# The last 128 rows of a gate's weights: in two early transfers of 16 partitions each, instead of in a late one of 128

## The chip, the cores and the metric

One core of a Trainium2 chip runs the kernel alone. The metric is the device time of one execution in microseconds (us), and lower is better. The core has five engines that compute or issue (TensorE, VectorE, ScalarE, GpSimd, SyncE) and 16 DMA engines that move data between the chip's memory (HBM) and the core's on-chip memory (SBUF, 128 partitions). Three runs of the kernel before took 242.82, 243.05 and 243.05 us; the median is 243.05 us.

## The reference

One decode step of a transformer block for four sequences (B = 4, one token each, D = 512), all in float32. A condition vector `c` sets six modulation vectors through one weight matrix `w_mod` (512 x 3072):

```python
mod = (_silu(c) @ w_mod).reshape(c.shape[0], 6, 1, -1)
sa, ca, ga, sb, cb, gb = (mod[:, 0], mod[:, 1], mod[:, 2], mod[:, 3], mod[:, 4], mod[:, 5])
h = _layernorm(x, axis=-1) * (1 + ca) + sa
x = x + ga * _A_ref(h, A_k_cache, A_v_cache, A_wq, A_wo)
h = _layernorm(x, axis=-1) * (1 + cb) + sb
x = x + gb * _B_ref(h, B_w1, B_w3, B_w2)
```

`_A_ref` is attention of 32 query heads over 8 key/value heads and a window of the last 2048 cached positions; `_B_ref` is the gated feed-forward layer `(silu(h @ w1) * (h @ w3)) @ w2` with 1792 hidden units. The gate `gb`, the last of the six, is what the change is about: `gb = silu(c) @ w_mod[:, 2560:3072]`, a product over 512 rows of weights that is needed only at the very end.

## The kernel before, in words

The kernel reads about 101 MB once and keeps nothing between executions. Nearly all of it comes in as transfers over all 128 partitions, issued by SyncE (`load`, L88) in an order written out by hand (L91 to L125). Each transfer has its own place in two big buffers `KV[0]`, `KV[1]` (128 x 16384 floats) and one smaller one, `WP`.

- **Start.** SyncE issues `t0_in` (the 16 columns of `c`, and the weights of `sa` and `ca`) into `T0`, which is the front of `KV[1]`; ScalarE's queue issues the first query weights `t1_in` and the 8 KB of `x_in`; SyncE then issues the keys and values of the first group, `KV[0]`. GpSimd writes constants with memsets (L128 to L139). VectorE and ScalarE make the layer norm of `x` and `silu(c)` (L174 to L188); the result `sc` is a 128 x 16 tile, four columns for each of the four blocks of 128 rows of `c`. TensorE multiplies it with `T0` (L302 to L306). When that is done (semaphore `pe` at 1) `KV[1]` is free and SyncE issues the second group's keys and values (L95, L96).
- **Attention.** TensorE, ScalarE and VectorE go through the eight groups two by two (L317 to L343). SyncE waits for the end of a group's work on a buffer (`x_done`, `qt_done`, `a_done`) before it issues the next transfer into it (L97 to L116).
- **Tail.** When the seventh group is done, SyncE issues the weights of `ga`, `sb`, `cb` (`wm_in`, L118) and a part of the feed-forward weights (L119). When the eighth is done it issues, one behind the other (L120 to L125), the rest of `w3` in two transfers, `gb_in` (the weights of `gb`, 512 rows laid out as 128 partitions x 4 blocks of 512 columns, 1024 KB) and `w2` in six transfers, cut so that the last ones are small (`W2_CUTS`, L18). TensorE computes `ga`, `sb`, `cb` (L380 to L385), then the feed-forward layer, and in between `gb` (L453 to L456): four products of a 128 x 4 block of `sc` with 128 x 512 weights, each into its own 32 rows of the bank `bM`. They are summed over the four blocks by a later product with `same` (L471 to L477). The last products with `w2` (L462 to L486), two VectorE operations (L488, L490) and a store (L492) end the kernel.

The bank `bM` is written three times: for `sa` and `ca`, for the attention's output (L353), which VectorE reads at L390, and for `gb`.

Of the kernel before, what the change touches and what calls it, by code (L numbers as in the profile page):

```python
# [5 lines left out]
AF = mybir.ActivationFunctionType  # L6
# [4 lines left out]
B, D, HQ, G, SK, DH, W, FF = 4, 512, 32, 8, 8192, 128, 2048, 1792  # L11
P = 128
# [2 lines left out]
EPS = 1e-5  # L15
CHUNKS = [(j, c) for c in range(4) for j in range(4) if c < 2 or j < 3]
HEAD = 8
W2_CUTS = [0, 4, 8, 10, 12, 13, 14]  # L18
PAIRS = G // 2

# [20 lines left out]
        return (self.sem, self.n)  # L41


def block_kernel(nc, x_in, t0_in, t1_in, kv_in, w_in, wm_in, f1_in, f2_in, gb_in, w2_in, out):
    T, v, s, gp, S = nc.tensor, nc.vector, nc.scalar, nc.gpsimd, nc.sync

    def sems(names):
        return [nc.alloc_semaphore(n) for n in names.split()]

    def sb(name, cols, rows=P):  # L50
        return nc.alloc_sbuf_tensor(name, (rows, cols), F32).ap()

    def bank(name):
        return nc.alloc_psum_tensor(name, (P, 512), F32).ap()

    (first,) = sems("first")
    A = Queue(nc, s, "act")
    V = Queue(nc, v, "dve")
    L = Queue(nc, gp, "pool")
    dx, dt0, dt1, dkv, dk, dva, dvb, dwo, dm, df1, df2a, df2b, dgb = sems("dx dt0 dt1 dkv dk dva dvb dwo dm df1 df2a df2b dgb")  # L60
    dw = sems(" ".join(f"dw{i}" for i in range(len(W2_CUTS) - 1)))
    z_ok, q_ok, p_ok, k_ok, va_ok, vb_ok, pt_ok, o_ok, ot_ok = sems("z_ok q_ok p_ok k_ok va_ok vb_ok pt_ok o_ok ot_ok")
    s_done, q_done, qt_done, pp_done, o_done, x_done, a_done, pe, last = sems("s_done q_done qt_done pp_done o_done x_done a_done pe last")
# [1 line left out]

    KV = [sb("KV0", 16384), sb("KV1", 16384)]
    WP = sb("WP", 8192)
    T0 = KV[1][:, : 16 + 4096]
    x_sb = sb("x_sb", 512, B)
    ident, same, eps = sb("ident", P), sb("same", B), sb("eps", 1)  # L70
    sc, e1, e2 = sb("sc", 16), sb("e1", 16), sb("e2", 16)
    hT, h2T = sb("hT", 16), sb("h2T", 16)
    Z = sb("Z", B * 28)
    q_sb, p_sb, o_sb, a_sb, y_sb, g_sb, u_sb, gb_sb = [sb(n, 512) for n in "q_sb p_sb o_sb a_sb y_sb g_sb u_sb gb_sb".split()]
# [10 lines left out]
    bS, bQ, bT, bP, bO, bX, bA, bM = [bank(n) for n in "bS bQ bT bP bO bX bA bM".split()]  # L85


    def load(dst, src, sem):  # L88
        S.dma_start(dst, src).then_inc(sem, 16)  # L89

    load(T0, t0_in, dt0)  # L91
    s.dma_start(WP[:, 4096:], t1_in).then_inc(dt1, 16)
# [27 lines left out]
    S.wait_ge(x_done, G)  # L120
    load(KV[1][:, :3072], f2_in[:, :3072], df2a)
    load(KV[1][:, 3072:6144], f2_in[:, 3072:], df2b)
    load(KV[1][:, 6144:8192], gb_in, dgb)
    for a, b, sem in zip(W2_CUTS[:-1], W2_CUTS[1:], dw):
        load(KV[1][:, 8192 + a * 512 : 8192 + b * 512], w2_in[:, a * 512 : b * 512], sem)  # L125


    l_eps = L.op(gp.memset(eps, EPS))  # L128
    t = L.op(gp.memset(ident, 0.0))
    L.wait(t)  # L130
# [48 lines left out]
    v_same = V.op(v.tensor_reduce(same, ident.rearrange("p (j i) -> p i j", i=32)[:, :B, :], axis=AX.X, op=ALU.add))  # L179

    A.wait((dt0, 16))
    t = A.op(s.activation(e1, T0[:, :16], AF.Exp, scale=-1.0))
    V.wait(t)
    t = V.op(v.tensor_scalar(e2, e1, 1.0, None, op0=ALU.add))
    V.wait(t)
    t = V.op(v.reciprocal(e2, e2))
    V.wait(t, (dt0, 16))
    t_sc = V.op(v.tensor_mul(sc, T0[:, :16], e2))  # L188

    A.wait((pe, 1))  # L190
    t_sa = A.op(s.copy(sa_sb, bM[32 : 32 + B, :]))
# [1 line left out]
    t = V.op(v.scalar_tensor_tensor(xs, bM[:B, :], 1.0, xc, op0=ALU.add, op1=ALU.mult))  # L193
# [60 lines left out]
    def mm(o, lhsT, rhs, start=True, stop=True):  # L254
        return T.matmul(o, lhsT, rhs, start=start, stop=stop, skip_group_check=True)  # L255
# [46 lines left out]
    T.wait_ge(V.sem, t_sc[1])  # L302
    for k in range(4):
        for i in range(2):
            ins = mm(bM[32 * i : 32 * i + B, :], sc[:, k * B : (k + 1) * B], T0[:, 16 + (2 * k + i) * 512 : 16 + (2 * k + i + 1) * 512], k == 0, k == 3)
    ins.then_inc(pe, 1)  # L306
    T.wait_ge(V.sem, t_h[1])
    for k in range(4):
        ins = T.transpose(bT[:, k * B : (k + 1) * B], h[:, k * P : (k + 1) * P], ident[:B, :B])
# [71 lines left out]
    for k in range(4):  # L381
        for i in range(3):
            at = (3 * k + i) * 512
            ins = mm(bX[32 * i : 32 * i + B, :], sc[:, k * B : (k + 1) * B], KV[0][:, at : at + 512], k == 0, k == 3)
# [3 lines left out]

    V.wait((pe, 3), t_ga)
    t = V.op(v.tensor_mul(ag, bM[:B, :], ga_sb))  # L390
    V.wait(t)
    t_x1 = V.op(v.scalar_tensor_tensor(x1, ag, 1.0, x_sb, op0=ALU.mult, op1=ALU.add, accum_out=st2[:, 0:1]))
    t_ss, t_r0, t_xc = stats(x1, t_x1, st2)
# [10 lines left out]
    for k in range(4):  # L404
        ins = T.transpose(bT[:, k * B : (k + 1) * B], h[:, k * P : (k + 1) * P], ident[:B, :B])
# [4 lines left out]
    def view(t_):  # L410
        return t_.rearrange("p (c j i) -> p c j i", c=4, j=4)
# [4 lines left out]
    for k in range(4):  # L416
        for j in range(4):
            at = 6144 + k * 2048 + j * 512
            ins = mm(bQ[32 * j : 32 * j + B, :], h2T[:, k * B : (k + 1) * B], KV[0][:, at : at + 512], k == 0, k == 3)
# [3 lines left out]
    for k in range(4):  # L423
# [5 lines left out]
        for j in range(3):  # L429
            at = k * 1536 + j * 512  # L430
            ins = mm(bA[32 * j : 32 * j + B, :], h2T[:, k * B : (k + 1) * B], KV[1][:, at : at + 512], k == 0, k == 3)
    ins.then_inc(pe, 1)
    A.wait((pe, 7))
    t = A.op(s.activation(view(eT), view(bP)[:, :, :, :B], AF.Exp, scale=-1.0))
    V.wait(t)
    t = V.op(v.tensor_scalar(dT, eT, 1.0, None, op0=ALU.add))
    V.wait(t)
    t = V.op(v.reciprocal(rT, dT))
# [7 lines left out]
    for c in range(4):  # L446
        ins = T.transpose(bS[:, c * P : c * P + 96], u_sb[:96, c * P : (c + 1) * P], ident[:96, :96])
# [3 lines left out]


    T.wait_ge(dgb, 16)  # L453
    for k in range(4):
        ins = mm(bM[32 * k : 32 * k + B, :], sc[:, k * B : (k + 1) * B], KV[1][:, 6144 + 512 * k : 6144 + 512 * (k + 1)])
    ins.then_inc(pe, 1)  # L456
    A.wait((pe, 10))
    t_gb = A.op(s.copy(gb_sb, bM))
    T.wait_ge(V.sem, t_hid[1])
    hw = view(hidT)  # L460
    w2 = KV[1][:, 8192 : 8192 + 14 * 512].rearrange("p (n m) -> p n m", n=14)
    for i in range(len(W2_CUTS) - 1):  # L462
        T.wait_ge(dw[i], 16)
        for n in range(W2_CUTS[i], W2_CUTS[i + 1]):
            jj, c = CHUNKS[n]
            if n < HEAD:
                ins = mm(bO[32 * (n % 4) : 32 * (n % 4) + B, :], hw[:, c, jj, :], w2[:, n, :], n < 4, n >= HEAD - 4)
                continue
            for j in range(4):
                ins = mm(bX[32 * j : 32 * j + B, :P], hw[:, c, jj, :], w2[:, n, j * P : (j + 1) * P], n == HEAD, n == 13)  # L470
        if i == 0:  # L471
            T.wait_ge(A.sem, t_gb[1])
            for j in range(4):
                ins = mm(bT[32 * j : 32 * j + B, :P], same, gb_sb[:, j * P : (j + 1) * P])
# [13 lines left out]
    t = V.op(v.tensor_mul(yt, bX[:, :P], gbJ))  # L488
# [8 lines left out]
def _layout(i):  # L497
    import numpy as np

    def a(t):  # L500
        return np.ascontiguousarray(t)

    k = i["A_k_cache"][:, :, SK - W :, :].reshape(B, G, NT, 512, DH)
    v = i["A_v_cache"][:, :, SK - W :, :].reshape(B, G, NT, 4, P, DH)
    k = k.transpose(1, 4, 2, 0, 3).reshape(G, P, 8192)
    v = v.transpose(1, 4, 2, 0, 3, 5).reshape(G, P, 8192)
    wm = i["w_mod"].reshape(4, P, 6, 512).transpose(1, 0, 2, 3)
    c = i["c"].reshape(B, 4, P).transpose(2, 1, 0).reshape(P, 16)
    wq = i["A_wq"].reshape(4, P, G, 512).transpose(2, 1, 0, 3).reshape(G, P, 2048)
    wo = i["A_wo"].reshape(G, R, P, D).transpose(0, 2, 1, 3).reshape(G, P, 2048)  # L510
    pairs = [[wo[2 * p], wo[2 * p + 1]] + ([wq[2 * p + 2], wq[2 * p + 3]] if p < 3 else [wo[6], wo[7]]) for p in range(4)]
    w1 = i["B_w1"].reshape(4, P, FF).transpose(1, 0, 2)
    w3 = i["B_w3"].reshape(4, P, FF).transpose(1, 0, 2)
    w2 = i["B_w2"].reshape(14, P, D)
    return {
        "x_in": a(i["A_x"].reshape(B, D)),
        "t0_in": np.concatenate([c, wm[:, :, 1::-1].reshape(P, 4096)], 1),
        "t1_in": np.concatenate([wq[0], wq[1]], 1),
        "kv_in": np.concatenate([k, v], 2),
        "w_in": np.stack([np.concatenate(p, 1) for p in pairs]),  # L520
        "wm_in": a(wm[:, :, 2:5]).reshape(P, 6144),
        "f1_in": np.concatenate([w1, w3[:, :, 1536:]], 2).reshape(P, 8192),
        "f2_in": a(w3[:, :, :1536]).reshape(P, 6144),
        "gb_in": a(wm[:, :, 5]).reshape(P, 2048),
        "w2_in": a(np.stack([w2[4 * j + c_] for j, c_ in CHUNKS], 1)).reshape(P, 14 * D),
    }

# [14 lines left out]
```

## Time and profile before

| | before |
|---|---|
| median of 3 runs | 243.05 us (242.82 to 243.05) |
| the profiled execution's own time | 243.12 us |
| its span, first to last instruction | 241.8 us |
| bytes moved by DMA | 101.33 MB, mean 419 GB/s over the span |
| TensorE busy with products | 136.2 us (56%) |
| VectorE, ScalarE, GpSimd busy | 38.6, 25.1, 1.7 us |
| mean granted TensorE clock | 0.852 |

The profiled execution took 1.3 us more than its span, and 0.07 us more than the median of the runs. A page of the profile has the busy shares of each engine, the chain of work that ended last, the costliest groups of instructions and the DMA queues; the trace can be asked for the same in any stretch of time. A DMA share of 1.00 in a stretch means 16 DMA engines busy all the time; transfers are counted where a packet starts, so that short stretches may read a little over 1. Queue q1 is SyncE's, q10 ScalarE's; the queues of the kind "instruction" carry the instructions themselves. The profile doesn't tell the 16 DMA engines apart.

### The profile page before, as it was taken

What the parts mean: (1) busy time and instruction counts of PE and PEld (TensorE: products, weight loads), DVE (VectorE), ACT (ScalarE), POOL (GpSimd) and SP (SyncE); (2) the same over time, 40 slices, a digit from 0 to 9 for tenths busy, and PEclk for the clock granted to TensorE, in tenths of its full rate; (3) what the DMA queues carried; (4) which work ended last, traced back from release to release, by engine and by line L of the source; (5) the groups of instructions that cost most, each with busy time, mean ns of one, the idle gap of its engine ahead of it and who ended that gap; (6) DMA issues with size and microseconds to landing.
All of it is one profiled execution on the core that took longest, in us unless ns stands there. A gap on an engine that the chain in (4) does not pass through costs nothing. (4 is left out here: it accounts for less than half of the span.)

```text
span 241.8 us, 2271 instructions
## 1 busy us (share of the span) xinstructions
PE 136.2 (56%) x940; PEld 37.3 (15%) x940; DVE 38.6 (16%) x126; ACT 25.1 (10%) x54; POOL 1.7 (1%) x14
## 2 busy tenths in 40 slices
PE   3004677817660387276723772667237768665964
PEld 0000121201210012112200121112001222111211
DVE  3003202202200022022000220220002222124122
ACT  2002002100120002001100020001001201123110
POOL 2000000000000000000000000000000000000000
PEclk9999959967996579987985798879858997995999
DMA  7998989899989898999898989998989999999992
GB/s 266 451 500 369 499 371 488 379 417 445 493 379 488 369 499 381 407 428 510 369 499 369 499 369 423 434 510 369 499 350 442 442 400 440 453 431 396 418 411 106
DMA packets 4044, 101.33 MB, mean 419 GB/s; under 512 B 452, under 2 KB 580, under 8 KB 1096
## 3 DMA queue, kind: packets, MB, share of 16 engines
q1 hardware_dynamic: 3888, 99.17, 95.6%
q10 hardware_dynamic: 152, 2.11, 2.1%
q8 instruction: 3, 0.05, 0.1%
q14 instruction: 1, 0.01, 0.0%
HBM read 101.20 MB, written 0.07 MB: 419 GB/s over the span
## 5 line engine op out<-in xcount | busy, mean ns | idle before, releaser
L255 PE MATMUL bS<-KV,Z 128*16 128x512 f32 x256 | 42.5, 824 | 38.8 <-PEq L258 38.8
L255 PE MATMUL bO<-KV,pT 128*16 128x512 f32 x256 | 31.9, 642 | 0.5
L255 PEld LDWEIGHTS bS<-KV,Z 128*16 128x16 f32 x256 | 9.1, 122 | 66.6 <-issue 66.6
L218 DVE TENSOR_REDUCE MX<-bS 128x1 f32<-128x512 f32 x8 | 5.5, 691 | 79.6 <-PE bS L255 79.6
L255 PE MATMUL bM<-KV,sc 128*4 128x512 f32 x24 | 7.3, 835 | 16.6 <-DVE sc L188 16.6
L367 ACT ACTIVATE p_sb<-bS,NB 128x512 f32<-128x512 f32 x8 | 5.5, 687 | 101.2 <-ACTq L358 101.2
L276 PE MATMUL bP<-ident,p_sb 128*128 128x128 f32 x32 | 5.0, 280 | 17.3 <-PEq L258 17.3
L255 PE MATMUL bA<-WP,oT 128*4 128x512 f32 x64 | 10.4, 728 | 5.2 <-PEq L258 5.2
L255 PEld LDWEIGHTS bO<-KV,pT 128*16 128x16 f32 x256 | 8.1, 105 | 22.9 <-issue 22.9
L372 ACT ACTIVATE o_sb<-bO,LB 128x512 f32<-128x512 f32 x8 | 5.5, 687 | 48.7 <-ACTq L358 48.7
L255 PE MATMUL bQ<-WP,hT 128*4 128x512 f32 x64 | 9.2, 648 | 0.6 <-DVE hT L197 0.6
L276 PE MATMUL bX<-ident,o_sb 128*128 128x128 f32 x32 | 5.0, 280 | 7.9 <-PEq L258 7.9
L244 DVE TENSOR_REDUCE oT<-bX 128x16 f32<-128x64 f32 x8 | 1.8, 224 | 44.0 <-PE bX L276 44.0
L276 PE MATMUL bT<-ident,q_sb 128*128 128x128 f32 x32 | 5.5, 298 | 3.6 <-PEq L258 3.6
L276 PEld LDWEIGHTS bP<-ident,p_sb 128*128 128x128 f32 x32 | 3.4, 140 | 24.4 <-issue 24.4
L276 PEld LDWEIGHTS bX<-ident,o_sb 128*128 128x128 f32 x32 | 3.4, 141 | 15.0 <-issue 15.0
L227 DVE COPY pT<-bP 128x256 f32<-128x256 f32 x8 | 3.4, 424 | 13.7 <-PE bP L276 13.7
L255 PE MATMUL bQ<-KV,h2T 128*4 128x512 f32 x32 | 5.3, 831 | 0.3 <-DVE h2T L408 0.3
L276 PEld LDWEIGHTS bT<-ident,q_sb 128*128 128x128 f32 x32 | 3.7, 150 | 8.3 <-issue 8.0
L255 PEld LDWEIGHTS bM<-KV,sc 128*4 128x4 f32 x24 | 1.0, 106 | 22.6 <-DVE sc L188 18.2
L255 PE MATMUL bX<-KV,sc 128*4 128x512 f32 x24 | 4.4, 592 | 0.0
L202 DVE TENSOR_REDUCE Z<-bT 128x16 f32<-128x64 f32 x8 | 1.8, 224 | 15.4 <-PE bT L276 15.1
(101 smaller groups left out, 68.0 us busy)
## 6 DMA issues: line engine op xcount, KB each, us to landing
WP<-w_in SPq DMA_DIRECT2D x3, 4096.0 KB, 18.9
KV<-kv_in SPq DMA_DIRECT2D x1, 4096.0 KB, 24.1
KV<-f_in SPq DMA_DIRECT2D x1, 4096.0 KB, 25.9
KV<-kv_in SPq DMA_DIRECT2D x1, 3072.0 KB, 30.9
KV<-wm_in SPq DMA_DIRECT2D x1, 3072.0 KB, 16.5
KV<-f_in SPq DMA_DIRECT2D x2, 1536.0 KB, 17.2
KV<-t_in SPq DMA_DIRECT2D x1, 2056.0 KB, 12.3
WP<-t_in ACTq DMA_DIRECT2D x1, 2048.0 KB, 12.5
```

What stands on the lines that cost most here:

```text
L202: v.tensor_reduce(Z.rearrange("p (b i) -> p b i", b=B)[:, :, 12 : 12 + R], bT.rearrange("p (r k i) -> p i r k", r=R, k=4)[:, :B], axis=AX. ...
L218: t = V.op(v.reduce_max(MX[:, 0:1], bS, axis=AX.X))
L227: v.tensor_copy(pT.rearrange("p (t b c r) -> p c b t r", t=NT, b=B, c=4), bP.rearrange("p (c b i) -> p c b i", c=4, b=B)[:, :, :, :16].rea ...
L244: V.op(v.tensor_reduce(oT.rearrange("p (r b) -> p r b", r=R), diag, axis=AX.X, op=ALU.add), ot_ok)
L255: return T.matmul(o, lhsT, rhs, start=start, stop=stop, skip_group_check=True)
L276: ins = T.transpose(dst[:, c * P : (c + 1) * P], src[:, c * P : (c + 1) * P], ident)
L367: A.op(s.activation(p_sb, bS, AF.Exp, bias=NB[:, 0:1], accum_out=SM[:, 0:1]), p_ok)
L372: A.op(s.mul(o_sb, bO, LB[:, 0:1]), o_ok)
```

## The change

The weights of `gb` have four blocks of 128 rows. The first three stay in `gb_in`, which is now 768 KB. The last block's 128 rows are cut into four sub-blocks of 32 rows, laid side by side (32 partitions x 2048 columns), and put on partitions 16 to 31 and 64 to 79 of a new tile `GC` (80 partitions x 2048 columns), the rest of which GpSimd sets to zero. GpSimd's own queue issues this at the start of the kernel, as two transfers of 16 partitions each (128 KB each). The source of each is written as four rows of four (of an array that has a fifth, unused row, so that the two can't be merged into one of sixteen). Ahead of them and behind them stands a transfer of 4 x 2 floats into an unused tile `GZ`.

The matching values of `c` are added to `t0_in`: 16 columns more (`cs`), zero outside those 32 partitions, so that `sc` has 32 columns. The four products with `GC` are placed behind those with `w_mod`'s middle part, into `bM`, after VectorE has read the attention's output from it. The three products that are left at the old place add to them. `w2` moves forward by 512 columns in `KV[1]`.

```diff
+SUB = 4
+BANDS = [16, 64]
+ROWS = [p for at in BANDS for p in range(at, at + 16)]
+C_IN = 16 + 4 * SUB
+W2_AT = 6144 + 1536
...
+    GC, GZ = sb("GC", SUB * 512, 80), sb("GZ", 4, 4)
+    T0 = KV[1][:, : C_IN + 4096]
...
-    load(KV[1][:, 6144:8192], gb_in, dgb)
+    load(KV[1][:, 6144:7680], gb_in, dgb)
...
+    t = L.op(gp.memset(GC, 0.0))
+    L.wait(t)
+    gp.dma_start(GZ[:, :2], gc_in[0, :4, :2]).then_inc(dgc, 16)
+    for e, at in enumerate(BANDS):
+        gp.dma_start(GC[at : at + 16], gc_in[4 * e : 4 * e + 4, :4]).then_inc(dgc, 16)
+    gp.dma_start(GZ[:, 2:], gc_in[0, :4, :2]).then_inc(dgc, 16)
     l_eps = L.op(gp.memset(eps, EPS))
...
-    t = A.op(s.activation(e1, T0[:, :16], AF.Exp, scale=-1.0))
+    t = A.op(s.activation(e1, T0[:, :C_IN], AF.Exp, scale=-1.0))
...
     t = V.op(v.tensor_mul(ag, bM[:B, :], ga_sb))
+    T.wait_ge(V.sem, t[1])
+    T.wait_ge(dgc, 64)
+    for m in range(SUB):
+        mm(bM[32 * m : 32 * m + B, :], sc[:80, 16 + m * B : 16 + (m + 1) * B], GC[:, m * 512 : (m + 1) * 512], True, m == 3)
...
     T.wait_ge(dgb, 16)
-    for k in range(4):
-        ins = mm(bM[32 * k : 32 * k + B, :], sc[:, k * B : (k + 1) * B], KV[1][:, 6144 + 512 * k : 6144 + 512 * (k + 1)])
+    for k in range(3):
+        ins = mm(bM[32 * k : 32 * k + B, :], sc[:, k * B : (k + 1) * B], KV[1][:, 6144 + 512 * k : 6144 + 512 * (k + 1)], False, True)
...
+    cs = np.zeros((P, SUB * B), c.dtype)
+    cs[ROWS] = i["c"].reshape(B, 512)[:, 384:].reshape(B, SUB, 32).transpose(2, 1, 0).reshape(32, SUB * B)
+    gc = np.zeros((8, 5, SUB * 512), c.dtype)
+    gc[:, :4] = i["w_mod"][384:, 5 * 512 :].reshape(SUB, 32, 512).transpose(1, 0, 2).reshape(8, 4, SUB * 512)
...
-        "gb_in": a(wm[:, :, 5]).reshape(P, 2048),
+        "gb_in": a(wm[:, :3, 5]).reshape(P, 1536),
+        "gc_in": gc,
```

Where the four products stand: TensorE's rows there before, from the products with `wm_in` to those of the feed-forward layer (tile out<-in, size, and the semaphores waited for).

```order
L255 MATMUL bX<-KV,sc 4x512 [waits dm]
L255 MATMUL bX<-KV,sc 4x512 x11
L405 MATMUL bT<-ident,h 128x4 [waits dve]
L405 MATMUL bT<-ident,h 128x4 x3
L255 MATMUL bQ<-KV,h2T 4x512 [waits df1,dve]
```

And the same place now:

```order
L267 MATMUL bX<-KV,sc 4x512 [waits dm]
L267 MATMUL bX<-KV,sc 4x512 x11
L267 MATMUL bM<-GC,sc 4x512 [waits dgc,dve]
L267 MATMUL bM<-GC,sc 4x512 x3
L421 MATMUL bT<-ident,h 128x4 [waits dve]
L421 MATMUL bT<-ident,h 128x4 x3
L267 MATMUL bQ<-KV,h2T 4x512 [waits df1,dve]
```

The four products, with a wait for `GC` (`dgc`) and for VectorE's reading of `bM`, stand between the two groups that followed each other before.

GpSimd's first rows before, behind its four built-in constants:

```order
L128 MEMSET eps 128x1
L129 MEMSET ident 128x128
```

And now:

```order
L134 MEMSET GC 80x2048
L136 DMA GZ<-gc_in 4x2
L138 DMA GC<-gc_in 16x1x2048 x2
L139 DMA GZ<-gc_in 4x2
L140 MEMSET eps 128x1
L141 MEMSET ident 128x128
```

One long memset and four transfers now stand ahead of every constant that GpSimd writes.

More of the change, by code (lines that the diff above doesn't have):

```diff
@@ L41, in op, with block_kernel @@
         return (self.sem, self.n)
-def block_kernel(nc, x_in, t0_in, t1_in, kv_in, w_in, wm_in, f1_in, f2_in, gb_in, w2_in, out):
+def block_kernel(nc, x_in, t0_in, t1_in, kv_in, w_in, wm_in, f1_in, f2_in, gb_in, gc_in, w2_in, out):
     T, v, s, gp, S = nc.tensor, nc.vector, nc.scalar, nc.gpsimd, nc.sync
@@ L59, in block_kernel @@
     L = Queue(nc, gp, "pool")
-    dx, dt0, dt1, dkv, dk, dva, dvb, dwo, dm, df1, df2a, df2b, dgb = sems("dx dt0 dt1 dkv dk dva dvb dwo dm df1 df2a df2b dgb")
+    dx, dt0, dt1, dkv, dk, dva, dvb, dwo, dm, df1, df2a, df2b, dgb, dgc = sems("dx dt0 dt1 dkv dk dva dvb dwo dm df1 df2a df2b dgb dgc")
     dw = sems(" ".join(f"dw{i}" for i in range(len(W2_CUTS) - 1)))
@@ L67, in block_kernel @@
     WP = sb("WP", 8192)
-    T0 = KV[1][:, : 16 + 4096]
+    GC, GZ = sb("GC", SUB * 512, 80), sb("GZ", 4, 4)
+    T0 = KV[1][:, : C_IN + 4096]
     x_sb = sb("x_sb", 512, B)
     ident, same, eps = sb("ident", P), sb("same", B), sb("eps", 1)
-    sc, e1, e2 = sb("sc", 16), sb("e1", 16), sb("e2", 16)
+    sc, e1, e2 = sb("sc", C_IN), sb("e1", C_IN), sb("e2", C_IN)
     hT, h2T = sb("hT", 16), sb("h2T", 16)
@@ L122, in block_kernel @@
     load(KV[1][:, 3072:6144], f2_in[:, 3072:], df2b)
-    load(KV[1][:, 6144:8192], gb_in, dgb)
+    load(KV[1][:, 6144:7680], gb_in, dgb)
     for a, b, sem in zip(W2_CUTS[:-1], W2_CUTS[1:], dw):
-        load(KV[1][:, 8192 + a * 512 : 8192 + b * 512], w2_in[:, a * 512 : b * 512], sem)
+        load(KV[1][:, W2_AT + a * 512 : W2_AT + b * 512], w2_in[:, a * 512 : b * 512], sem)
+    t = L.op(gp.memset(GC, 0.0))
[4 more added lines that the diff above has]
+    gp.dma_start(GZ[:, 2:], gc_in[0, :4, :2]).then_inc(dgc, 16)
     l_eps = L.op(gp.memset(eps, EPS))
@@ L187, in block_kernel @@
     V.wait(t, (dt0, 16))
-    t_sc = V.op(v.tensor_mul(sc, T0[:, :16], e2))
+    t_sc = V.op(v.tensor_mul(sc, T0[:, :C_IN], e2))
     A.wait((pe, 1))
@@ L304, in block_kernel @@
         for i in range(2):
-            ins = mm(bM[32 * i : 32 * i + B, :], sc[:, k * B : (k + 1) * B], T0[:, 16 + (2 * k + i) * 512 : 16 + (2 * k + i + 1) * 512], k == 0, k == 3)
+            ins = mm(bM[32 * i : 32 * i + B, :], sc[:, k * B : (k + 1) * B], T0[:, C_IN + (2 * k + i) * 512 : C_IN + (2 * k + i + 1) * 512], k == 0, k == 3)
     ins.then_inc(pe, 1)
@@ L460, in block_kernel @@
     hw = view(hidT)
-    w2 = KV[1][:, 8192 : 8192 + 14 * 512].rearrange("p (n m) -> p n m", n=14)
+    w2 = KV[1][:, W2_AT : W2_AT + 14 * 512].rearrange("p (n m) -> p n m", n=14)
     for i in range(len(W2_CUTS) - 1):
@@ L516, in _layout @@
         "x_in": a(i["A_x"].reshape(B, D)),
-        "t0_in": np.concatenate([c, wm[:, :, 1::-1].reshape(P, 4096)], 1),
+        "t0_in": np.concatenate([c, cs, wm[:, :, 1::-1].reshape(P, 4096)], 1),
         "t1_in": np.concatenate([wq[0], wq[1]], 1),
```

## The prediction

> **What bounds the kernel now.** I read the page's DMA part first, since so much is moved, then the chain that ended last, then the last microseconds in short windows.
>
> ```profile
> DMA  7998989899989898999898989998989999999992
> ...
> DMA packets 4044, 101.33 MB, mean 419 GB/s; under 512 B 452, under 2 KB 580, under 8 KB 1096
> ...
> q1 hardware_dynamic: 3888, 99.17, 95.6%
> ...
> q8 instruction: 3, 0.05, 0.1%
> q14 instruction: 1, 0.01, 0.0%
> ```
>
> The first row is the busy share of the 16 DMA engines in 40 slices: no slice but the first and the last falls under 8 tenths. TensorE is busy 56% of the span, so this kernel is bound by its transfers. The q1 row gives an engine's pace: 99.17 MB in 0.956 x 241.8 us x 16 engine-microseconds is 26.8 KB a microsecond (thousand bytes) for one engine. So 16,384 B cost an engine 0.61 us, 32,768 B 1.22 us.
>
> Do the engines ever run dry in the middle? SyncE waits for TensorE before most issues, but the issues are early. The page's issue rows give the time from issue to landing:
>
> ```profile
> WP<-w_in SPq DMA_DIRECT2D x3, 4096.0 KB, 18.9
> ...
> KV<-gb_in SPq DMA_DIRECT2D x1, 1024.0 KB, 20.8
> ...
> KV<-kv_in SPq DMA_DIRECT2D x7, 32.3
> ```
>
> 4,096 KB take 16 engines 9.8 us at that pace, and landed after 18.9: such a transfer stood some 9 us behind others. The queue holds many microseconds of work at each issue, so TensorE's speed doesn't matter there. What counts is how many bytes each engine has to move until the end. The chain says the same of the end:
>
> ```profile
> 212.29 26.78 DMA KV<-w_in
> 239.06 0.04 issue
> 239.11 0.45 PE bX L255 x8
> 239.57 0.30 DVE yt L488
> 239.90 0.29 DVE y L490
> ```
>
> The last `w2` transfer, issued at 212.29, lands at 239.06; a product, two VectorE operations and the store follow, and the change touches none of them. So an earlier landing is an earlier end, one for one. Now the windows before that landing (us, busy time by engine, granted clock, DMA share, GB/s):
>
> ```profile
> 236.50:237.00 0.50, 0.38 (x16) 0.32 (x16) 0.50 (x1) 0.00 (x0) 0.00 (x0) 1.00 0.93 328
> 237.00:237.50 0.50, 0.50 (x20) 0.11 (x8) 0.12 (x1) 0.00 (x0) 0.00 (x0) 1.00 0.26 98
> 237.50:238.00 0.50, 0.21 (x12) 0.13 (x12) 0.00 (x0) 0.00 (x0) 0.00 (x0) 1.00 0.19 74
> 238.00:238.50 0.50, 0.50 (x18) 0.20 (x13) 0.00 (x0) 0.00 (x0) 0.00 (x0) 1.00 0.14 53
> 238.50:239.00 0.50, 0.39 (x8) 0.10 (x8) 0.00 (x0) 0.00 (x0) 0.00 (x0) 1.00 0.02 8
> ```
>
> This is the row set that matters. From 237.5 to 238.0 three engines' worth is still busy (0.19 x 16 = 3.0; 74 GB/s is 2.8 engines), from 238.0 to 238.5 two (53 GB/s is 2.0). The others are done at about 237.1. So **two engines are late by about 1.5 us and a third by half of that**, and thirteen stand idle while the kernel waits. What makes them late stands in the DMA view of four stretches (30 to 40, 90 to 100, 210 to 220, 236 to 239 us; the last column is the share of 16 engines):
>
> ```profile
> q8 instruction: 1, 0.02, 0.6%
> ```
> ```profile
> q14 instruction: 1, 0.01, 0.2%
> ```
> ```profile
> q8 instruction: 1, 0.02, 0.7%
> ```
> ```profile
> q8 instruction: 1, 0.02, 2.3%
> ```
>
> Each is one packet of instructions, and takes one engine for 0.006 x 16 x 10 = 1.0 us, 0.3, 1.1 and 0.023 x 16 x 3 = 1.1 us. An engine hit by one never catches up, because its queue never empties. Two long refills and a short one fit two very late engines and a third one; the fourth refill came when the thirteen were done or nearly so.
>
> **The change, part by part.** *Bytes at the end.* `gb_in` loses 512 of 2048 columns: 262,144 B. If they were spread evenly over 16 engines, as the windows suggest (thirteen end together), each engine loses 16,384 B: **-0.61 us on every engine**. Every engine gains 16 columns of `c`: 8,192 B / 16 = 512 B, **+0.02 us**.
>
> *Bytes at the start.* The same 262,144 B come in by GpSimd's queue. No transfer of that queue is in the trace, so which engines it uses is bounded by two cases. If each of the two uses four engines, following its source's four rows, eight engines get 32,768 B (+1.22 us) and eight get nothing. If each is spread over all sixteen, every engine gets 16,384 B (+0.61 us). I take the first for the forecast. Then eight engines end up at -0.61 + 0.02 = -0.59 us, eight at +0.63. The loaded eight, if on time before, end at 237.1 + 0.6 = 237.7, which is 0.3 us ahead of the late two even at their new time, 238.6 - 0.6 = 238.0. So if both late engines are among the unloaded eight, the landing moves by -0.59, whole.
>
> *Four more completions.* Four transfers each report their end by small writes, perhaps on every engine, and two move 32 B. Nothing shows their price. The tail bounds it: 2 KB pieces there still ran at 53 GB/s on two engines, full pace, so a small packet costs under 2,048 / 26,800 = 0.08 us; four cost 0 to 0.3 us. I take 0.05, near the lower end, since they carry bytes and not kilobytes. Sum: -0.61 + 0.02 + 0.05 = **-0.54 us**.
>
> *GpSimd at the start.* Rows of the timeline (start, us, engine, line):
>
> ```profile
> 0.73 0.38 SPq L89 DMA_DIRECT2D KV<-t_in  x1
> ...
> 1.16 26.73 SPq L89 DMA_DIRECT2D KV<-kv_in  x2
> ...
> 1.43 0.52 POOL L135 MEMSET y_sb<- 128x512 f32 x1
> ...
> 17.85 0.67 DVE L175 TENSOR_REDUCE st<-x_sb 4x1 f32<-4x512 f32 x1 [14.82 <-DMA x_sb<-x_in]
> ...
> 19.58 0.29 ACT L156 ACTIVATE st<-st,eps 4x1 f32<-4x1 f32 x1
> ...
> 21.25 6.27 PE L255 MATMUL bM<-KV,sc 128*4 128x512 f32 x16 [16.65 <-DVE sc L188]
> ```
>
> `GC` has four times `y_sb`'s columns: about 4 x 0.52 = 2.1 us of memset, then four issues, 0.4 us each by SyncE's row, or up to three times that. So `eps`, `ident` and the zeros come 4 to 7 us later, at up to 10 us. The first that need them are ScalarE at 19.58 (`eps`) and TensorE, whose zeroing of `bA` must be over by 21.25. Cost nothing; without that cover it would delay the start by up to 7 us. The wider `silu(c)` (32 columns for 16) adds some 0.02 us to four operations. They lie ahead of `pe` at 1, on which SyncE's second `kv_in` waits (its two issues end at 27.9), while the queue holds the first until about 32: nothing. The early transfers make the loaded engines 1.2 us later with `T0`, which is needed at 20 us and can't come later than `x_in`'s 17.85 by that much: nothing.
>
> *TensorE in the tail.*
>
> ```profile
> 211.27 4.01 PE L255 MATMUL bX<-KV,sc 128*4 128x512 f32 x22
> ...
> 216.03 0.68 DVE L390 TENSOR_TENSOR ag<-bM,ga_sb 4x512 f32<-4x512 f32 x1 [5.26 <-ACT ga_sb L387]
> ...
> 220.26 0.58 PE L405 MATMUL bT<-ident,h 4*128 4x4 f32 x4 [4.98 <-DVE h L398]
> ...
> 231.86 1.04 PE L255 MATMUL bM<-KV,sc 128*4 128x512 f32 x8
> ...
> 235.32 1.04 PE L255 MATMUL bO<-KV,hidT 128*4 128x512 f32 x8 [1.16 <-DMA KV<-w_in]
> ```
>
> The four products wait for VectorE's `ag` (until 216.71) and then take 1.04 us, as the same four did for `gb`; at half the clock twice that. They end at 217.8 to 218.8, and what is queued behind them, the transposes of `h`, waits for VectorE until 220.26 anyway: hidden in 4.98 us of idle time. Without that cover, TensorE still has 1.16 us to spare before the second `w2` piece. At the old place three products replace four; TensorE waits for `w2` soon after, so this gains nothing. The wait for `dgc` is on transfers issued some 200 us earlier.
>
> **A rule against it.** The row with the refills says that late engines are late by where refills hit. The Trainium skill ("DMA: Bandwidth & Descriptors", section "Latency and other measured facts") has it that DMA engines 7 and 15 are usually slower than the rest, by a guess about descriptor rings. By its section "The descriptor swizzle", partitions 16 to 31 and 64 to 79 belong to engines 4 to 11: by both, engine 7 would be loaded, and the sum would be +0.68, not -0.54. No row here names an engine, so the trace neither agrees nor disagrees.
>
> **Rivals.**
>
> *A late engine is among the loaded eight.* Then it has -0.61 + 0.02 + 1.22 + 0.05 = +0.68 us, and the landing with it: 243.05 + 0.68 = 243.7. This decides as soon as one of the two is loaded. By mere count, both are unloaded with 8/16 x 7/15 = 0.23. But both were hit by packets of one queue (q8), and engines that serve one purpose are likelier neighbours than scattered; neighbours are both in or both out at about even odds. I can't do better from the rows.
>
> *It doesn't unbalance anything.* GpSimd's two transfers go over all sixteen: +0.61 at the start, -0.61 at the end, and the small terms remain: +0.07, so 243.1. For it: nothing shows how that queue spreads 16 rows. Against: nothing either, beyond the four-row form of its source. The Trainium skill's same page ("Why a DMA increments its semaphore by 16 and not by 1") knows both: as many engines as divide both sides' outer sizes, here four, but for some of GpSimd's direct copies all 16. No run here shows which.
>
> *A refill hits a loaded engine.* The refill at 236 to 239 hit an engine outside the late two, late enough to do no harm. If that engine is loaded, its data ends 0.6 us later and the refill falls into it: 237.1 + 0.6 + 1.5 = 239.2 against 238.6 before, about +0.5: 243.55. The program's code is also longer, so refills may come at other places.
>
> **How the numbers follow.** The profiled execution's own time is 243.12 us; -0.54 gives 242.58. The median of the runs is 0.07 lower: 243.05 - 0.54 = 242.51, rounded **242.5**. Chances: forecast 0.55, late engine loaded 0.20, spread evenly 0.10, refill on a loaded engine 0.10, anything else 0.05. What this kernel's measurement can tell from no change is about 0.2%, 0.49 us, and the forecast lies just beyond it: with the small writes at up to 0.3 us, three tenths of its chance fall within. Faster: 0.7 x 0.55 and part of the rest, 0.42. Within 0.2%: 0.3 x 0.55 + 0.08, 0.25. Slower: 0.20 + 0.10 and the rest, 0.33. Range: from 242.3 (a little under -0.59, for the runs' own 0.23 us) to 243.75, which takes in the second case. The likeliest case alone: 242.3 to 242.75.
>
> **What would show it.** Right: the last landing near 238.5, and in the windows after 237 about eight engines busy until 237.7 and two until 238.0; the four `GC` products between 216.7 and 219; the transposes of `h` still at about 220. A share of 0.02 to 0.19 that lasts beyond 238.6 means a late engine carries more. Windows like before's, with both ends 0.0 to 0.1 us later, mean an even spread. Wrong altogether: an idle DMA slice in the middle, or a chain that ends on TensorE or GpSimd.

## The result

| | before | changed |
|---|---|---|
| median of the runs on one chip | 243.05 us (242.82 to 243.25, 6 runs) | 246.01 us (245.41 to 246.79, 6 runs) |
| the profiled execution's own time | 243.12 us | 245.99 us |
| its span | 241.8 us | 244.7 us |
| last `w2` landing | 239.06 us | 241.93 us |

The changed kernel takes 1.0124 times as long, 95% interval 1.0112 to 1.0136: slower by 3.0 us. The forecast was 242.5 us, with a range to 243.75. The last landing alone moved by 241.93 - 239.06 = 2.87 us, so the loss lies ahead of it.

### The profile page after: what moved, and what is told of

It reads as the page before. It is cut to its first block, busy times and chain, and to the rows that moved or that the text cites. A ratio compares the mean times of both kernels' runs of the same rounds, so it can differ in the third digit from the quotient of the medians.

```text
span 244.7 us, 2289 instructions
## 1 busy us (share of the span) xinstructions
PE 137.3 (56%) x946; PEld 37.9 (15%) x946; DVE 38.8 (16%) x126; ACT 25.1 (10%) x54; POOL 5.9 (2%) x19
## 2 busy tenths in 40 slices
DMA packets 4268, 101.34 MB, mean 414 GB/s; under 512 B 644, under 2 KB 772, under 8 KB 1416
## 5 line engine op out<-in xcount | busy, mean ns | idle before, releaser
L288 PE MATMUL bP<-ident,p_sb 128*128 128x128 f32 x32 | 5.9, 317 | 17.3 <-PEq L270 17.3
L267 PE MATMUL bM<-KV,sc 128*4 128x512 f32 x22 | 6.8, 813 | 15.2 <-DVE sc L200 15.2
L288 PEld LDWEIGHTS bP<-ident,p_sb 128*128 128x128 f32 x32 | 3.9, 159 | 24.5 <-issue 24.5
L267 PE MATMUL bA<-y_sb 128*128 128x512 f32 x2 | 2.1, 1142 | 7.0 <-POOL x1J L151 7.0
```

The source lines that it names most:

```text
L288: ins = T.transpose(dst[:, c * P : (c + 1) * P], src[:, c * P : (c + 1) * P], ident)
```

## The profile after

First the page's DMA part of the changed kernel.

```profile
DMA  7999999989999999999999998999989999999993
...
DMA packets 4268, 101.34 MB, mean 414 GB/s; under 512 B 644, under 2 KB 772, under 8 KB 1416
...
q1 hardware_dynamic: 3888, 98.91, 95.3%
...
q0 software_dynamic: 224, 0.26, 0.3%
```

Queue q0 is GpSimd's, and new: 0.26 MB. The sum of the bytes is 101.34 MB for 101.33. No slice of the DMA row is idle, yet the mean rate fell from 419 to 414 GB/s. So the engines are busy as before and move less in the time. The chain that ended last, changed kernel:

```profile
213.99 27.94 DMA KV<-w_in
241.93 0.04 issue
241.97 0.45 PE bX L267 x8
```

It is the chain of before, later. GpSimd is not on it, and TensorE stands on it only with 0.64 us ahead of SyncE's issues and with the last products behind the landing, as before. The windows ahead of the landing (same columns as in the prediction, the DMA share and the GB/s last):

```profile
239.00:239.50 0.50, 0.26 (x8) 0.05 (x8) 0.22 (x1) 0.00 (x0) 0.00 (x0) 1.00 0.99 377
239.50:240.00 0.50, 0.50 (x16) 0.27 (x16) 0.47 (x1) 0.00 (x0) 0.00 (x0) 1.00 0.88 315
240.00:240.50 0.50, 0.43 (x12) 0.11 (x8) 0.00 (x0) 0.00 (x0) 0.00 (x0) 1.00 0.61 234
240.50:241.00 0.50, 0.30 (x12) 0.30 (x16) 0.00 (x0) 0.00 (x0) 0.00 (x0) 1.00 0.28 107
241.00:241.50 0.50, 0.48 (x20) 0.14 (x12) 0.00 (x0) 0.00 (x0) 0.00 (x0) 1.00 0.07 25
```

Before, the share was down to 0.26 at 237.0 to 237.5. Now all engines are still busy at 239.0 (share 0.99 to 239.5). That isn't one late engine. A single row can say it for all sixteen: from 234 us on, share times length is the time for which an average engine stays busy, so 234 plus that product is the **mean end** of the engines. Such a row of before, and one of the changed kernel:

```profile
234.00:239.50 5.50, 3.58 (x72) 1.09 (x64) 0.69 (x1) 0.27 (x1) 0.00 (x0) 1.00 0.60 232
```
```profile
234.00:242.00 8.00, 5.68 (x86) 1.83 (x90) 1.44 (x3) 0.85 (x2) 0.00 (x0) 1.00 0.81 322
```

Before: 234 + 0.60 x 5.50 = 237.30 us. Changed: 234 + 0.81 x 8.00 = 240.48. (The share has two digits, so a mean end is good to 0.03 to 0.05 us.) The average engine ends 3.2 us later, with the same bytes. Where did it lose them? The mean rate from 40 to 200 us, before and changed:

```profile
40.00:200.00 160.00, 89.81 (x632) 26.04 (x628) 22.33 (x80) 14.65 (x30) 0.00 (x0) 0.83 1.00 430
```
```profile
40.00:200.00 160.00, 94.07 (x645) 27.35 (x641) 21.66 (x77) 13.99 (x28) 0.00 (x0) 0.81 1.00 430
```

Both 430 GB/s: nothing is lost there. The DMA view of 8 to 34 us, before and changed (packets, MB, share of 16 engines):

```profile
q1 hardware_dynamic: 228, 10.49, 93.2%
```
```profile
q1 hardware_dynamic: 193, 9.20, 91.4%
...
q0 software_dynamic: 193, 0.26, 3.2%
```

Dividing bytes by busy time gives the **pace** of an engine on SyncE's transfers. Before: 10.49 MB / (0.932 x 26 x 16 us) = 27.1 KB/us. Changed: 9.20 / (0.914 x 416) = 24.2, or 11% less. At 27.1 those 9.20 MB would have taken 340 engine-microseconds instead of 380; 40 / 16 engines = 2.5 us of the 3.2 are in these rows alone. Nor did the engines run dry there: their share from 8 to 34 us is 1.05 in the changed kernel. The single packets of the trace say when: one of 65,536 B takes 2,418 ns in the kernel before. In the changed one the median is 3,124 ns from 8 to 14 us, 2,734 and 2,794 in the next two stretches of six, and 2,420 from 32 us on. The rows of `GC` are under way from 9.8 to 28.1 us. While they are, **all sixteen engines are slow**, though at most eight carry such a row: of the 80 packets of 65,536 B that start from 8 to 26 us, some five for each engine, not one took less than 2,581 ns.

The rest of the start, in rows of the changed kernel's timeline:

```profile
0.73 1.80 POOL L134 MEMSET GC<- 80x2048 f32 x1 [0.29 <-POOLq L556]
...
2.84 0.66 POOL L136 DMA_DIRECT2D GZ<-gc_in  x1 [0.31 <-POOL GC L134]
3.50 1.17 POOL L138 DMA_DIRECT2D GC<-gc_in  x2
4.66 0.54 POOL L139 DMA_DIRECT2D GZ<-gc_in  x1
...
7.00 1.22 PE L267 MATMUL bA<-y_sb 128*128 128x512 f32 x1 [7.00 <-POOL x1J L151]
```
```profile
20.73 0.67 DVE L187 TENSOR_REDUCE st<-x_sb 4x1 f32<-4x512 f32 x1 [17.70 <-DMA x_sb<-x_in]
...
22.45 0.29 ACT L168 ACTIVATE st<-st,eps 4x1 f32<-4x1 f32 x1
...
30.10 0.33 SPq L95 DMA_DIRECT2D KV<-kv_in  x1
```

The memset and the issues delay GpSimd's constants to 7.0 us; ScalarE wants `eps` at 22.45. That cost nothing. But what waits for `x_in` starts 2.9 us later than before (20.73 for 17.85), and SyncE's next issue comes at 30.10 for 27.57, while the queue still holds work (the share of 1.05 above). The tail, changed kernel:

```profile
218.56 0.68 DVE L402 TENSOR_TENSOR ag<-bM,ga_sb 4x512 f32<-4x512 f32 x1 [6.09 <-ACT ga_sb L399]
...
219.29 1.04 PE L267 MATMUL bM<-GC,sc 80*4 80x512 f32 x8 [1.47 <-DVE ag L402]
...
222.79 0.40 PE L421 MATMUL bT<-ident,h 4*128 4x4 f32 x4 [2.46 <-DVE h L414]
```

The four products (eight records) follow `ag`, take 1.04 us, and TensorE still idles 2.46 us before the transposes: hidden, as forecast.

## The experiments

Nine kernels (one of them twice, 5 and 9), all made from the changed one and measured against the kernel before on the same chip. Pace and mean end are worked out as above; the last column is what the last landing lies behind the mean end, the **lag** of the latest engine.

| kernel | median us (runs) | ratio to before, 95% interval | pace 8 to 34 us, KB/us | mean end, us | last landing, us | lag, us |
|---|---|---|---|---|---|---|
| before | 243.05 (6) | | 27.1 | 237.30 | 239.06 | 1.8 |
| changed | 246.01 (6) | 1.0124 [1.0112, 1.0136] | 24.2 | 240.48 | 241.93 | 1.5 |
| 1: partitions 0 to 31 | 243.32 (10) | 1.0011 [1.0001, 1.0022] | 27.1 | 237.41 | 238.90 | 1.5 |
| 2: ScalarE's queue | 246.96 (4) | 1.0163 [1.0146, 1.018] | 25.0 | 240.18 | 242.97 | 2.8 |
| 3: ScalarE's queue, other partitions | 244.23 (4) | 1.0049 [1.0032, 1.0066] | 27.1 | 237.29 | 240.23 | 2.9 |
| 4: one transfer, 128 partitions | 243.25 (10) | 1.0008 [0.9998, 1.0017] | 27.0 | 237.36 | 239.16 | 1.8 |
| 5: steered | 243.73 (12) | 1.0023 [1.0011, 1.0035] | 27.0 | 237.41 | 238.30 | 0.9 |
| 6: without the weights | 242.43 (10) | 0.9977 [0.9968, 0.9986] | 27.1 | 236.70 | 238.30 | 1.6 |
| 7: one of two moved | 244.33 (4) | 1.0059 [1.0044, 1.0073] | 25.6 | 238.69 | 240.25 | 1.6 |
| 8: steered, another pair | 243.73 (5) | 1.0033 [1.002, 1.0046] | 27.0 | 237.45 | 239.57 | 2.1 |
| 9: as 5, once more | 243.0 (1) | | 27.0 | 237.52 | 238.93 | 1.4 |
| 10: steered, a third pair | 243.73 (8) | 1.002 [1.0008, 1.0032] | 27.1 | 237.45 | 239.80 | 2.4 |

Median and profile are of different executions, so a row's median and landing need not go together.

Two theories stood at first. **Place:** an engine that writes partitions which in the big transfers belong to another engine slows the others while its rows are under way. (Rows that their partitions' own engines carry are called **at home** below.) **Queue:** GpSimd's own queue disturbs all engines, wherever the rows go. The trace gave a hint to the first: packets of one engine follow each other within some 10 ns, so that the rows can be followed engine by engine, but for places where two engines end at the same moment. The first transfer of `GC` went by the same four engines that carry the four rows of `x_in`, the second by four others. The Trainium skill ("DMA: Bandwidth & Descriptors", section "The descriptor swizzle") gives partitions 16 to 31 to engines 4 to 7 and 64 to 79 to 8 to 11 in a transfer over 128 partitions, and the section "Why a DMA increments its semaphore by 16 and not by 1" lets a transfer of ScalarE's queue that uses four engines take the lowest ones. By both, the first transfer was carried by the wrong four, and the second too if its four are engines 4 to 7, the next in order. The trace doesn't name engines, so this is a guess at the pairs; the experiments decide (experiment 7 takes the second transfer alone).

### 1. The same transfers, to other partitions

```diff
-BANDS = [16, 64]
+BANDS = [0, 16]
```

> Changed kernel with one number pair changed: the two 16-row transfers go to partitions 0 to 15 and 16 to 31, not 16 to 31 and 64 to 79. Theory P (place): the two transfers were carried by DMA engines other than those that normally write these partitions, and that slows all transfers while their rows are under way; here the first two groups of four engines write their usual partitions, so from 8 to 34 us the mean is about 435 to 441 GB/s as before (441) and not 402, and the time is 242.5 to 243.9 us. Theory Q (queue): any rows of GpSimd's queue slow the rest, wherever they land; the mean stays near 402 GB/s and the time near 246.

Its DMA view of 8 to 34 us and its row of the end:

```profile
q1 hardware_dynamic: 225, 10.30, 91.5%
```
```profile
234.00:239.50 5.50, 3.61 (x72) 1.09 (x64) 0.78 (x2) 0.27 (x1) 0.00 (x0) 1.00 0.62 238
```

10.30 / (0.915 x 416) = 27.1 KB/us, and a mean end of 237.41: the slowing is gone, with the same queue, the same number and size of rows, the same zeroing and waits. One line of numbers took 2.7 us off the median (246.01 to 243.32). The queue theory falls here.

### 2. The changed kernel's partitions, on ScalarE's queue

```diff
-    L.wait(t)
-    gp.dma_start(GZ[:, :2], gc_in[0, :4, :2]).then_inc(dgc, 16)
+    s.wait_ge(L.sem, t[1])
...
-        gp.dma_start(GC[at : at + 16], gc_in[4 * e : 4 * e + 4, :4]).then_inc(dgc, 16)
-    gp.dma_start(GZ[:, 2:], gc_in[0, :4, :2]).then_inc(dgc, 16)
+        s.dma_start(GC[at : at + 16], gc_in[4 * e : 4 * e + 4, :4]).then_inc(dgc, 16)
...
```

> Changed kernel with the two transfers issued on ScalarE's queue instead of GpSimd's, to the same partitions 16 to 31 and 64 to 79; the two small ones into GZ are left out. Theory P: still slow, 8 to 34 us at 405 GB/s or less, time 245.5 or more. Theory Q: 8 to 34 us at 435 to 441 GB/s; time 243.0 to 244.6, since one group of four engines then carries all 256 KB (2.4 us more each, less 0.6).

```profile
q1 hardware_dynamic: 216, 9.97, 96.0%
```
```profile
234.00:243.50 9.50, 6.98 (x99) 1.91 (x90) 2.12 (x7) 0.85 (x2) 0.00 (x0) 1.00 0.65 260
```

The pace is 9.97 / (0.960 x 416) = 25.0 KB/us and the mean end 234 + 0.65 x 9.5 = 240.18, 2.9 us late: slow without GpSimd's queue. The rows came later here, behind ScalarE's other transfer, and so did the slowing: large packets took 2,418 ns until 17 us, and a median of 2,958 from 32 to 38 us. The rows start from 19.4 to 42.0 us with a pause between 29.4 and 34.2, and the fifteen large packets that lie in this pause (started from 30.4 to 31.9) took 2,418 to 2,426 ns again. The slowing lasts as long as the rows.

### 3. ScalarE's queue, partitions 0 to 15 and 32 to 47

As experiment 2, and `BANDS = [0, 32]`, two bands that are both meant to be at home with the four engines that ScalarE's queue uses.

> As the run before it, but to partitions 0 to 15 and 32 to 47. Theory P: no slowdown, 435 to 441 GB/s from 8 to 34 us, 243.0 to 244.6 us (one group of four engines carries 2.4 us more). Theory Q: the same. A slowdown here speaks against both: it would be the form of the transfers (16 rows of 8 KB from four rows of four) whatever the queue and the place.

```profile
q1 hardware_dynamic: 225, 10.30, 91.5%
```

The pace is full again and the mean end is that of before (237.29). The 1.2 us that it is slower are lag: both transfers go by one group of four engines (`x_in`'s, by the trace), which end late. So the place holds on both queues.

### 4. One transfer over 128 partitions, early, on GpSimd's queue

```diff
+    gp.dma_start(GC, gc_in).then_inc(dgc, 16)
...
+    mm(bM[96 : 96 + B, :], sc[:, 12:16], GC)
...
```

These stand in the places of the memset, the four transfers and the four products; `GC` is 128 x 512, and the 16 extra columns of `c` are gone.

> Last 128 weight rows early on GpSimd's queue, but as one transfer over all 128 partitions (512 columns), with one product in the new place. Theory P: no slowdown; bytes per engine as before, so 243.0 to 243.2 us and 435 to 441 GB/s from 8 to 34 us. Theory Q: the same bytes by the same queue, so 8 to 34 us near 402 GB/s and 245 us or more.

It measured no difference. Every engine carries its own 16 KB early instead of late. Nothing is gained and nothing is lost: in this queue that never empties, early and late are the same.

### 5. The changed kernel's partitions, steered to other engines

The small transfer ahead has 16 rows instead of 4.

```diff
-    GC, GZ = sb("GC", SUB * 512, 80), sb("GZ", 4, 4)
+    GC, GZ = sb("GC", SUB * 512, 80), sb("GZ", 16, 16)
...
-    gp.dma_start(GZ[:, :2], gc_in[0, :4, :2]).then_inc(dgc, 16)
+    gp.dma_start(GZ[:, :8], gc_in[:4, :4, :8]).then_inc(dgc, 16)
...
-    gp.dma_start(GZ[:, 2:], gc_in[0, :4, :2]).then_inc(dgc, 16)
+    gp.dma_start(GZ[:, 8:], gc_in[:4, :4, :8]).then_inc(dgc, 16)
```

> Changed kernel, same two transfers to partitions 16 to 31 and 64 to 79, but the two small transfers are 16 rows of 8 floats (sources of four rows of four, like the big ones) instead of 4 rows of 2. Theory P with steering: small transfers of 4 rows did not move GpSimd's choice of engines on, those of 16 rows do; then the second and third group of four engines carry the two bands, which they normally write: no slowdown (435 to 443 GB/s from 8 to 34 us) and the forecast comes true if the two late engines are not in these groups: 242.4 to 242.8; if one of them is, 243.5 to 243.9. Rival: the choice of engines has nothing to do with it and these partitions are slow for 16-row transfers anyhow: about 402 GB/s and 246 us.

```profile
q1 hardware_dynamic: 224, 10.23, 90.9%
```
```profile
234.00:239.50 5.50, 3.68 (x73) 1.09 (x64) 1.27 (x3) 0.27 (x1) 0.00 (x0) 1.00 0.62 239
```

Full pace. In the trace the rows go by two groups of four engines, and neither is the one that carries `x_in`'s rows: the choice of engines moved on. This pair with experiment 1 is the proof: there the same choice of engines wrote other partitions, here the same partitions are written by other engines, and either puts the loss away. So it is neither the engines nor the partitions, but the pairing. Its windows before the end:

```profile
236.50:237.00 0.50, 0.28 (x8) 0.00 (x0) 0.00 (x0) 0.00 (x0) 0.00 (x0) 1.00 0.78 295
237.00:237.50 0.50, 0.42 (x16) 0.32 (x16) 0.00 (x0) 0.00 (x0) 0.00 (x0) 1.00 0.61 234
237.50:238.00 0.50, 0.48 (x16) 0.11 (x8) 0.00 (x0) 0.00 (x0) 0.00 (x0) 1.00 0.19 70
238.00:238.50 0.50, 0.27 (x14) 0.11 (x8) 0.00 (x0) 0.00 (x0) 0.00 (x0) 1.00 0.00 0
```

This is close to the picture that the prediction drew: some ten engines from 237.0 to 237.5 (0.61 x 16), three until 238.0, and a landing at 238.30. That execution took 242.46 us. But the twelve runs go from 242.46 to 244.1, most of them near 243.8, and the median is slower than before.

### 6. All of it but the two transfers of weights

This kernel leaves the last 128 rows of weights out of the gate.

```diff
-    for e, at in enumerate(BANDS):
-        gp.dma_start(GC[at : at + 16], gc_in[4 * e : 4 * e + 4, :4]).then_inc(dgc, 16)
...
```

> Changed kernel without the two 16-row transfers; memset, small transfers, 32 columns of c and the products stay. The gate then leaves out the last 128 rows of its weights. Theory P: nothing is slow, every engine has 16,384 B less at the end: 0.61 less, 0.02 more for c and up to 0.05 for the small transfers: 242.4 to 242.55, and 441 GB/s from 8 to 34 us. Rival: GpSimd's memset, its queue or the small transfers themselves cost what was lost (then 244 or more).

```profile
234.00:239.00 5.00, 3.44 (x64) 1.09 (x64) 0.88 (x2) 0.00 (x0) 0.00 (x0) 1.00 0.54 207
```

The mean end is 234 + 0.54 x 5 = 236.70, or 0.60 us earlier than before, where 16,384 B less per engine had been put at 0.61. The median is 0.57 lower (242.43 for 243.00 on that chip). So the memset, the two small transfers, the wider `c` and the four products cost next to nothing together.

### 7. One band at home, one not

```diff
-BANDS = [16, 64]
+BANDS = [0, 64]
```

> Changed kernel with bands 0 to 15 and 64 to 79: by Theory P the first transfer (first group of four engines) is at home and the second is not, so about half of the loss: 244.0 to 245.2 us, and 8 to 34 us at 415 to 430 GB/s; the slow stretch begins only with the second transfer's rows, after some 16 us. Rival (the loss is all or nothing, or comes from the first transfer alone): 243.3 or 246.

The changed kernel's window of 8 to 16 us, and then three of this one:

```profile
8.00:16.00 8.00, 1.07 (x2) 0.00 (x0) 0.00 (x0) 0.00 (x0) 0.00 (x0) 1.00 1.10 403
```

```profile
8.00:16.00 8.00, 1.08 (x2) 0.00 (x0) 0.00 (x0) 0.00 (x0) 0.00 (x0) 1.00 1.12 479
16.00:24.00 8.00, 1.32 (x4) 0.23 (x6) 2.51 (x10) 1.43 (x5) 0.00 (x0) 1.00 1.05 405
24.00:34.00 10.00, 6.13 (x30) 1.43 (x26) 1.82 (x4) 1.17 (x2) 0.00 (x0) 1.00 0.98 404
```

With the first band at home, the first stretch runs at 479 GB/s for 403 in the changed kernel (483 in the kernel before), and the slowing begins with the second transfer's rows. The mean end is 238.69, 1.4 us late: a little under half of the changed kernel's 3.2. So it goes transfer by transfer, and each of the changed kernel's two was away from home.

### 8. Steered, partitions 16 to 31 and 80 to 95

A small transfer of 16 rows ahead of each of the two, meant to bring them to the second and the fourth group.

```diff
-BANDS = [16, 64]
+BANDS = [16, 80]
...
-    gp.dma_start(GZ[:, :2], gc_in[0, :4, :2]).then_inc(dgc, 16)
     for e, at in enumerate(BANDS):
+        gp.dma_start(GZ[:, 8 * e : 8 * e + 8], gc_in[:4, :4, :8]).then_inc(dgc, 16)
         gp.dma_start(GC[at : at + 16], gc_in[4 * e : 4 * e + 4, :4]).then_inc(dgc, 16)
-    gp.dma_start(GZ[:, 2:], gc_in[0, :4, :2]).then_inc(dgc, 16)
...
```

> As the first of these four, but bands 16 to 31 and 80 to 95, with a small 16-row transfer ahead of each big one, so that by Theory P the second and the fourth group of four engines carry them at home: no slowdown. The run with bands 0 to 15 and 16 to 31 had no landing as late as a loaded late engine would have, so the two late engines are in the third or fourth group. If they are in the third: 242.4 to 242.8; if one is in the fourth: 243.5 to 243.9.

Full pace, so the place holds for a third pair of groups. But the lag is 2.1 us, and the gain is gone.

### 9 and 10. What makes the steered kernels spread

Both ask whether the spread is one of late engines (theory L) or of a slowing as a whole (theory M). The ninth is experiment 5 once more. The tenth is meant for the third and fourth group:

```diff
-BANDS = [16, 64]
+BANDS = [64, 80]
...
     gp.dma_start(GZ[:, :8], gc_in[:4, :4, :8]).then_inc(dgc, 16)
+    gp.dma_start(GZ[:, 8:], gc_in[:4, :4, :8]).then_inc(dgc, 16)
...
```

> The steered placement (partitions 16 to 31 and 64 to 79) once more, for a second profile, since its 12 runs spread from 242.46 to 244.1 us. Theory L: the spread is one of late engines; which engines an instruction refill delays differs from execution to execution, and where a loaded one is hit, the last landing of w2 comes at 239.4 or later, with one to three engines busy alone in the last microsecond, while the mean from 8 to 34 us is 437 to 443 GB/s as in the first profile and from 40 to 200 us 430. Theory M: some executions are slowed as a whole, as by writes away from home; then the mean from 8 to 34 us is below 430 in an execution above 243.5 us, and the windows at the end fall together for all engines. An execution below 242.8 us would tell nothing.

> Partitions 64 to 79 and 80 to 95, with both 16-row small transfers ahead, so that the third and the fourth group of four engines carry the rows, each on its own partitions. Theory P (place of the rows against the engines): 437 to 443 GB/s from 8 to 34 us, no slowing. On the late engines: if they are the same engines in every execution and lie in the fourth group (as the second pair with that group suggested, median 243.73 and two late engines in its profile), the median is 243.6 to 243.9 with a small spread; if which engine is late differs between executions (theory L), single runs reach from 242.5 to 244.1, as for the second and third group. A median under 242.6 would mean that neither group holds a late engine as a rule.

The ninth took 243.0 us, with full pace: it lies between the cases and tells little. The tenth ran at 242.68 once and at 243.64 to 243.87 seven times. Its profile is of a run at 243.87, and its windows before the end read:

```profile
237.50:238.00 0.50, 0.50 (x20) 0.22 (x16) 0.38 (x1) 0.00 (x0) 0.00 (x0) 1.00 0.38 127
238.00:238.50 0.50, 0.34 (x8) 0.04 (x8) 0.00 (x0) 0.00 (x0) 0.00 (x0) 1.00 0.17 66
238.50:239.00 0.50, 0.44 (x16) 0.32 (x16) 0.00 (x0) 0.00 (x0) 0.00 (x0) 1.00 0.13 49
239.00:239.50 0.50, 0.48 (x16) 0.11 (x8) 0.00 (x0) 0.00 (x0) 0.00 (x0) 1.00 0.09 33
```

From 238.0 to 239.5 three engines, then two, then one or two work alone (0.17, 0.13 and 0.09 x 16 = 2.7, 2.1 and 1.4), while the pace at the start was full and the mean end 237.45: late engines, and not a slowing as a whole. Theory M falls for this execution. Whether the engine that is hit is a loaded one can be followed for the refill near 34 us. In experiment 10 a row of 8,192 B starts at 30.386 us, lasts 0.3, two packets of 65,536 B follow at 2.42 us each, and at 35.531 the refill starts on that engine: it is a loaded one. In experiment 8 the same sum leads from a row at 29.879 over one packet to the refill at 32.599: loaded too. In experiments 5 and 9 the refills at 33.969 and 34.791 fall on engines that carried no row from 12.5 us on, when every loaded engine still had some to carry, and so does experiment 1's at 34.315. The executions took 243.87 and 243.73 (loaded), 242.46, 243.0 and 242.97 (not loaded), with last landings at 239.80 and 239.57, and at 238.30, 238.93 and 238.90. That fits theory L in five of five profiles, though what was late at 238.93 in experiment 9 isn't shown. It isn't shown that the other runs of experiment 5 near 243.8 have the same reason: they have no profile.

## Why the prediction was wrong, point by point

- **The step that failed** is the cost of the bytes at the start. "Eight engines get 32,768 B (+1.22 us) and eight get nothing", and of the start, "The early transfers make the loaded engines 1.2 us later". Both give the early rows a price on the engines that carry them, and none to the others. The runs show a second price: carried by engines that don't own the partitions, these 256 KB make every engine slower while they are under way (2,581 ns and more for packets of 2,418), and the mean end moves by 3.2 us; with other partitions (experiment 1) or other engines (experiment 5) it moves by 0.1. The sum had no term for it, not even as a bound, and no rival had it. The text bounded that transfer's engines, though no transfer of that queue was in the trace, but not what else it might do.
- **16,384 B per engine at the end, -0.61 us:** right. Experiment 6 measured -0.60 in the mean end and -0.57 in the median.
- **The small terms, +0.07:** too small to tell, as forecast; experiment 6 has the columns, the memset and two of the four completions in its -0.57.
- **Four engines for each transfer, eight loaded:** right. The trace shows each transfer's rows on four engines, and the even spread falls.
- **Hidden work:** right on both places. GpSimd's constants were ready at 7.0 us, and the four products ended 2.46 us ahead of what stands behind them. But the start of what waits for `x_in` moved by 2.9 us, where the prediction allowed 1.2 for the loaded engines: the same missing term.
- **The rivals.** "A late engine is among the loaded eight" was put at 243.7, and the forecast at 242.5. In the changed kernel neither can be seen, since 3 us lie over them. In the steered kernels both can: 242.46, 242.55 and 242.68 at the one end, and 243.73 as the median of three pairs. The price was right, and the mechanism fits the executions at 243.73 and 243.87 that were followed, but the chances were off: with steering the second case is the commoner one. The 242.46 is one end of a spread and doesn't make the forecast right. It also isn't one engine by nature. The refill near 34 us hit a loaded engine in two profiles of steered kernels and spared them in two.
- **The refill on a loaded engine** had been looked for at the end of the kernel. It matters at 33 to 36 us, since a queue that never empties hands a delay on to the end. There it costs its engine more than its own 1.0 to 1.1 us: the packet of 65,536 B behind it took 2,886 ns for 2,418, in the kernel before as well (1.03 + 0.47 = 1.5 us, just as late as the prediction had read its two late engines).
- **The Trainium skill's rule on engines 7 and 15.** With it the prediction got +0.68, which is 243.73, and that is the median of experiment 5. But runs of the same kernel at 242.46 and 242.55, which should have that engine loaded, speak against a fixed late engine. No trace names an engine.
- **The tests named** would have told it: neither forecast nor late engine nor even spread fits windows that are full until 239.5. They show all engines late, a case that wasn't on the list.

Why the writes slow all sixteen engines, and not only the two groups whose partitions are involved, stays open. The Trainium skill ("SBUF — State Buffer", section "SBUF: two separate sides") names contention on the DMA ports where several DMA engines write to them. The runs agree that the place decides. That section by itself doesn't say why an engine which neither carries such a row nor owns its partitions slows down, as the packets of all sixteen show. Who owns which partitions isn't in the traces either; the runs show only which pairings are slow (changed, 2, and one of 7's two) and which aren't (1, 3, 5, 8, 10), and theory "place" had forecast each of them.

None of the nine beats the kernel before with the whole work done. Moving bytes early didn't lower the mean end; with every band at home it stays within about 0.2 us of before (237.29 to 237.52 for 237.30). All that was left to win is lag.

## What to carry to other kernels

In a kernel bound by transfers, ask of a transfer over a part of the partitions not only how many engines carry it, but whether they are those that write these partitions in the big transfers; check it in the pace of the *other* queues' packets while it runs. The mean end of the engines (share times length from a point at which all are still busy) and the lag of the last one tell a slower stream from an uneven one in one row each. Shifting bytes between engines could gain no more than the lag here (1.8 us before, 0.9 at best), and lost it again where a refill hit an engine that was given more (2.1 and 2.4).

## What the runs showed of the hardware that was not expected

- Rows of 8 KB to 16 partitions each, 256 KB in all, slowed packets of 65,536 B on all engines from 2,418 ns to a median of 2,734 to 3,124 ns while they were under way (pace 27.1 to 24.2 KB/us; 25.0 on ScalarE's queue), when the carrying engines and the partitions didn't match. At home the same rows slowed nothing (27.0 to 27.1).
- Behind a small transfer of 4 rows of 8 B, the next transfer of GpSimd's queue went by the four engines that carry `x_in`'s rows; behind one of 16 rows of 32 B it went by four others.
- One refill of 16 KB near 34 us takes 1.0 to 1.1 us of its engine, and the packet of 65,536 B behind it 2,886 ns for 2,418 (in experiment 8 the packet behind it is one of `GC`'s rows, with 774 ns for 309). In two profiles it went to an engine with 32 KB more to carry; these executions took 0.7 to 1.4 us more than those of experiments 5 and 9.
